# A decode attention layer on one core: the value product as 64 probability columns by 512 V columns in two column groups

## The chip, the cores and the metric

The kernel runs on one core of one Trainium2 chip. The metric is the device time of one execution in microseconds (us); lower is better.

## The reference

One decode step of an adaLN transformer block: 8 batch rows, one token each, model width 512, 32 query heads of width 128 over 8 key/value heads, and a window of W = 2048 cached positions. All data are fp32.

```
mod = (silu(c) @ w_mod) -> sa, ca, ga, sb, cb, gb
h = layernorm(x) * (1 + ca) + sa
q = h @ wq                              # 8 x 32 heads x 128
k, v = last 2048 positions of the caches # 8 x 8 heads x 2048 x 128
p = softmax(q k^T * 128**-0.5)
x = x + ga * ((p v) @ wo)
h = layernorm(x) * (1 + cb) + sb
x = x + gb * (relu(h @ w1 + b1)**2 @ w2 + b2)
```

The caches are large (the windows read are 67 MB of K and 67 MB of V), and each value of them is used for only 4 query heads.

## The kernel before

Everything that comes from DRAM passes through four SBUF slots of 4 MB each. `loads` lists the transfers in order: two pieces of w_mod, two of wq, then for each batch row b the tiles K(b,0), V(b-1,0), K(b,1), V(b-1,1), each 4 key/value heads of one batch row, and at the end wo in two loads, w1 and w2. `pump` issues the next load on SP as soon as a slot is free, and `done` frees a slot: after the scores for a K tile, after the value product for a V tile. The order of work on each engine is the order of the code (a manual schedule), so an instruction that waits holds everything behind it on its engine.

A batch row b goes through these steps, two batch rows overlapping:

- `turn` (line 287, DVE): a K tile is transposed in 32x32 blocks in its slot, in four pieces.
- `scores` (line 297, PE): 16 products for each K tile, stationary 32 columns of the spread queries, moving 512 columns of K, output in column group x of 32 partitions.
- `rows` and `maximum` (lines 309 to 326, DVE): scores to rows, maximum of each head. `exponent` (line 332, ACT): exponentials and their row sums.
- `divisor` (line 344 on PE, line 348 on DVE): the sums of a head over partitions, and their reciprocal rz. `spread` (line 356, ACT): the probabilities times rz, each repeated four times, to prd.
- `turn_p` (line 366 on PE, line 367 on DVE): prd transposed, and masked into pT, where the columns (x, r) of one j hold the 4 query heads r of each of the 4 key/value heads x, and zeros elsewhere.
- `weighted` (line 378 on PE, line 388 on ACT): the value product. A V tile has on each of 128 partitions (x, i) 64 positions j of 128 values. One product takes 32 columns of pT (two positions of 16 columns) as stationary operand and 256 columns of V (the same two positions) as moving operand; the output of 32 x 256 holds the wanted sums where both belong to the same position, and others beside them that are not used. 32 products go in turn to the four column groups of 32 output partitions, eight accumulating in each. ACT copies the result to o_sb.
- `gather` (line 396 on PE, lines 404 and 407 on DVE): products with the selection matrix sel4 add the wanted quarters over partitions and halves u; DVE picks the head's place and adds to oT.

The loop over b calls them as follows (shortened; every `turn` is one of four pieces):

```
turn(b,0,0); divisor(b-1); spread(b-1); gather(b-2); turn(b,0,1)
turn_p(b-1,0..1); turn(b,0,2); turn_p(b-1,2..3); turn(b,0,3)
scores(b,0); weighted(b-1,0)          # for b = 1 in the other order
turn(b,1,0..3); fill(b+1); scores(b,1)
rows(b); maximum(b); exponent(b); weighted(b-1,1)
```

After the last row come the output projection (lines 453 to 472: first half of wo by 512 columns, second half by 128), the second norm (h2T at line 142), the MLP (line 494 with w1, lines 505 to 507, line 516 with w2) and the result (lines 524 to 526). Before the loop stand the modulation (line 221), wq (line 243) and the small constants, sel4 (line 205) among them.

Of the kernel before, what the change touches and what calls it, by code (L numbers as in the profile page):

```python
# [8 lines left out]
F32 = mybir.dt.float32  # L9
# [9 lines left out]
def tile_adaln_cached_attention_mlp(  # L19
# [14 lines left out]
    nc = tc.nc  # L34
    P = 128
# [13 lines left out]
    consts = ctx.enter_context(tc.tile_pool(name="consts", bufs=1))  # L49
    work = ctx.enter_context(tc.tile_pool(name="work", bufs=2))  # L50
    ps_s = ctx.enter_context(tc.tile_pool(name="ps_s", bufs=1, space=bass.MemoryType.PSUM))
    ps_t = ctx.enter_context(tc.tile_pool(name="ps_t", bufs=2, space=bass.MemoryType.PSUM))
    ps_o = ctx.enter_context(tc.tile_pool(name="ps_o", bufs=2, space=bass.MemoryType.PSUM))
# [66 lines left out]
    def done(*keys):  # L120
        for k in keys:
            free.append(held.pop(k))
        pump()
# [4 lines left out]
    one = consts.tile([P, P], F32, name="ident")  # L128
# [4 lines left out]
    sel = consts.tile([P, P], F32, name="sel")  # L133
# [18 lines left out]
    def bank(name="m_ps"):  # L152
        return ps_m.tile([P, 512], F32, name=name, tag="m_ps")
# [47 lines left out]
    nc.vector.tensor_reduce(own, one.rearrange("p (x q r) -> p x r q", x=4, q=4), axis=AX.X, op=ALU.add)  # L201
    same = consts.tile([P, 4, 4, 8], F32, name="same")
    nc.vector.tensor_copy(same, own[:, :, None, :].to_broadcast([P, 4, 4, 8]))
    sel4 = consts.tile([P, 32, 4], F32, name="sel4")
    nc.vector.tensor_copy(sel4, sel[:, :32, None].to_broadcast([P, 32, 4]))
    qb = [consts.tile([P, 32, 4, 8], F32, name=f"qb{i}") for i in range(2)]
    for t in qb:
        nc.gpsimd.memset(t, 0.0)
# [8 lines left out]
    for kc in range(NQ):  # L217
        wm = slot(("mod", kc // 2), 6 * D)[:, kc % 2, :].rearrange("p (m q n) -> p m q n", m=6, q=NQ)
        for i in range(2):
            for q in range(NQ):  # L220
# [4 lines left out]
                    start=(kc == 0),  # L225
                    stop=(kc == NQ - 1),
# [12 lines left out]
    for kc in range(NQ):  # L239
        w = slot(("wq", kc // 2), HQ * DH)[:, kc % 2, :]  # L240
        for t in range(2):
            for x in range(4):
# [4 lines left out]
                    start=(kc == 0),  # L247
                    stop=(kc == NQ - 1),
# [4 lines left out]
    for t in range(2):  # L253
# [3 lines left out]
        for x in range(4):  # L257
# [4 lines left out]
                start=True,  # L262
                stop=True,
# [19 lines left out]
    S_, S2_, NM_, PR_, RZ_, PT_, O_ = ({} for _ in range(7))  # L283
# [88 lines left out]

    def weighted(b, t):
        v = slots[held["V", b, t]]
        o = ps_o.tile([P, 2, P], F32, name="o_ps")
        for m in range(32):
            n, q, u = m // 8, m // 2 % 4, m % 2
            nc.tensor.matmul(  # L378
                o[32 * (m % 4) : 32 * (m % 4) + 32].rearrange("p u d -> p (u d)"),
                PT_[b][:, n, 2 * q + t, 2 * u : 2 * u + 2, :].rearrange("p u r -> p (u r)"),  # L380
                v[:, 256 * m : 256 * m + 256],
                start=(m < 4),
                stop=(m >= 28),
            )
        done(("V", b, t))
        if t == 0:
            O_[b] = work.tile([P, 2, 2, P], F32, name="o_sb")
        nc.scalar.copy(O_[b][:, t], o)  # L388

    def gather(b):  # L390

        o = O_.pop(b)
        pg = bank()
        for t in range(2):
            for u in range(2):
                nc.tensor.matmul(  # L396
                    pg[64 * t : 64 * t + 64, :P],
                    sel4[:, 16 * u : 16 * u + 16, :].rearrange("p n u -> p (n u)"),
                    o[:, t, u, :],
                    start=(u == 0),  # L400
                    stop=(u == 1),
                )
        og = work.tile([P, 4, 32], F32, name="og")
        nc.vector.tensor_mul(  # L404
            og, pg[:, :P].rearrange("p (q i) -> p q i", q=4), m4[:, :, None].to_broadcast([P, 4, 32])
        )
        nc.vector.tensor_reduce(oT[:, :, b], og.rearrange("p q i -> p i q"), axis=AX.X, op=ALU.add)

    for b in range(B + 1):
# [5 lines left out]
        if b > 1:  # L415
            gather(b - 2)
# [12 lines left out]
        if b == 1:  # L429
            weighted(0, 0)  # L430
        if b < B:
            scores(b, 0)
        if b > 1:
            weighted(b - 1, 0)
# [11 lines left out]
        if b > 0:  # L446
            weighted(b - 1, 1)
    gather(B - 1)


    wo_ps = ps_s.tile([P, D], F32, name="s_ps")
    for i in range(16):
# [4 lines left out]
            start=(i < 4),  # L457
            stop=(i >= 12),
# [11 lines left out]
    for i in range(16, 32):  # L470
        for q in range(NQ):
# [4 lines left out]
                start=False,  # L476
                stop=(i == 31),
# [14 lines left out]
    for kc in range(NQ):  # L492
        for g in range(NQ):
# [4 lines left out]
                start=False,  # L498
                stop=(kc == NQ - 1),
            )  # L500
    r = work.tile([P, 32, FC], F32, name="relu", tag="a")
# [12 lines left out]
    for f in range(FC):  # L514
        for q in range(NQ):
# [4 lines left out]
                start=False,  # L520
                stop=(f == FC - 1),
# [41 lines left out]
```

## Time and profile before

| what | value |
|---|---|
| median of 3 runs | 393.99 us (393.91 to 394.86) |
| the profiled execution | 394.03 us, its span in the profile 392.2 us |
| busy: PE, DVE, ACT | 254.6, 213.8, 42.0 us |
| HBM read | 164.77 MB, 420 GB/s over the span |
| value product, line 378 | 1024 instructions, 59.7 us busy |
| scores, line 297 | 512 instructions, 120.9 us busy |
| turning K, line 287 | 64 instructions, 144.0 us busy |

PE is TensorE's matmuls, PEld its weight loads, DVE VectorE, ACT ScalarE, SPq the queue that issues the large loads. A row of the timeline reads: start, duration (both us), engine, line, operation, output<-input, partitions x elements, and in brackets the engine's idle time ahead of it with what ended that. Each fp32 product of the code is two matmul instructions in the profile. A row with x64 merges 64 neighbouring instructions; its duration runs from the first start to the last end. A row that groups a line's instructions (with a bar) has the busy us, the mean ns of one, and the idle time before them. A row with "min/median/max" has one line's durations in ns.

### The profile page before, as it was taken

The numbers are of one execution on the slowest core, as the hardware profiler recorded it, in microseconds if no ns is written. First come the engines' busy times: TensorE is split into PE (matmuls) and PEld (weight loads), VectorE is DVE, ScalarE is ACT, GpSimd is POOL, SyncE is SP. The second block draws the span as 40 slices with busy tenths as digits, with TensorE's granted clock in tenths as the row PEclk, the third lists the DMA queues.
The fourth block names the chain that finished last, engine by engine and source line by source line (L and its number), as shares of the span: only waits on it lengthen the run. The fifth ranks groups of instructions, "written<-read, shape, count | busy, mean of one in ns | idle before, by whom it ended". The sixth has DMA issues, their size and how long they took to land.

```text
span 392.2 us, 4985 instructions
## 1 busy us (share of the span) xinstructions
PE 254.6 (65%) x2224; PEld 112.9 (29%) x2224; DVE 213.8 (55%) x228; ACT 42.0 (11%) x88; POOL 4.7 (1%) x12
## 2 busy tenths in 40 slices
PE   0554808678966693849484939394849384984965
PEld 0211302051231332224332522143224221452423
DVE  2420299399394939283928491939293927230022
ACT  1300100030030002000200120003000300140000
POOL 4000000000000000000000000000000000000000
PEclk9998768969977988789578967797788879997869
DMA  8999999999999999999999999999999999999994
GB/s 333 429 428 426 431 441 438 431 434 438 426 431 426 428 426 428 428 433 434 429 434 433 438 427 428 434 433 428 426 428 434 424 431 426 438 429 412 433 417 170
DMA packets 6997, 165.15 MB, mean 421 GB/s; under 512 B 824, under 2 KB 1088, under 8 KB 1472
## 3 DMA queue, kind: packets, MB, share of 16 engines
q1 hardware_dynamic: 6768, 164.69, 98.1%
q8 instruction: 17, 0.28, 0.3%
q10 hardware_dynamic: 144, 0.13, 0.1%
q14 instruction: 4, 0.03, 0.0%
q0 software_dynamic: 64, 0.01, 0.0%
HBM read 164.77 MB, written 0.07 MB: 420 GB/s over the span
## 4 chain that ended last, share of the span: by engine, by line
DMA 55%; DVE 23%; PE 20%; issue 0%; ACT 0%; DVEq 0%; ACTq 0%
DMA slot<-in_A_k_cache_dram 37%; DVE slot L287 20%; PE s_ps L297 16%; DMA slot<-in_B_w_dram 8%; DMA slot<-in_A_v_cache_dram 6%; DMA xc_in<-in_xc_dram 3%; PE m_ps L221 2%; PE o_ps L378 2%; DVE pT L367 1%; PE t_ps L366 1%; PE t_ps L516 0%; DVE s L309 0%; DVE s L313 0%; DVE mx L318 0%; DVE e_sb L148 0%
## 5 line engine op out<-in xcount | busy, mean ns | idle before, releaser
L287 DVE STREAM_TRANSPOSE slot<-slot 128x2048 f32<-128x2048 f32 x64 | 144.0, 2284 | 43.4 <-DMA slot<-in_A_k_cache_dram 43.3
L297 PE MATMUL s_ps<-slot,qb 128*32 128x512 f32 x512 | 120.9, 1092 | 71.1 <-DVE slot L287 70.5
L297 PEld LDWEIGHTS s_ps<-slot,qb 128*32 128x32 f32 x512 | 24.2, 135 | 147.3 <-issue 79.0
L378 PE MATMUL o_ps<-slot,pT 128*32 128x256 f32 x1024 | 59.7, 381 | 0.8 <-DMA slot<-in_A_v_cache_dram 0.8
L378 PEld LDWEIGHTS o_ps<-slot,pT 128*32 128x32 f32 x1024 | 45.4, 112 | 29.1 <-issue 18.4
L366 PE MATMUL t_ps<-ident,prd 128*128 128x128 f32 x128 | 25.2, 348 | 17.3 <-ACT prd L356 9.5
L309 DVE STREAM_TRANSPOSE s<-s_ps 128x512 f32<-128x512 f32 x8 | 5.7, 717 | 54.1 <-PE s_ps L297 54.1
L366 PEld LDWEIGHTS t_ps<-ident,prd 128*128 128x128 f32 x128 | 18.5, 177 | 23.1 <-ACT prd L356 22.4
L356 ACT ACTIVATE prd<-pr,rz 128x512 f32<-128x512 f32 x32 | 20.5, 710 | 9.4 <-DVE rz L348 9.4
L332 ACT ACTIVATE pr<-s,nm 128x512 f32<-128x512 f32 x8 | 5.8, 722 | 142.7 <-DVE nm L326 142.7
L367 DVE TENSOR_TENSOR pT<-t_ps,m 128x512 f32<-128x512 f32 x32 | 20.2, 670 | 0.7 <-PE t_ps L366 0.6
L388 ACT COPY o_sb<-o_ps 128x256 f32<-128x256 f32 x16 | 5.8, 362 | 121.7 <-PE o_ps L378 121.7
L243 PE MATMUL t_ps<-slot,h1T 128*32 128x512 f32 x64 | 11.6, 889 | 10.2 <-DMA slot<-in_A_wq_dram 10.2
L255 DVE STREAM_TRANSPOSE qT<-t_ps 128x512 f32<-128x512 f32 x2 | 1.4, 717 | 19.0 <-PE t_ps L243 19.0
L274 DVE TENSOR_TENSOR qb<-qrep,block 128x512 f32<-128x512 f32 x8 | 9.0, 1124 | 2.1 <-ACT qrep L266 2.1
L158 PE MATMUL m_ps<-xsum,sel 128*128 128x1 f32 x2 | 0.6, 363 | 13.9 <-DVE xsum L181 13.9
L344 PE MATMUL m_ps<-z,same 128*128 128x1 f32 x16 | 3.3, 273 | 9.1 <-ACT pr L332 9.1
L453 PE MATMUL s_ps<-slot,oT 128*32 128x512 f32 x32 | 5.6, 864 | 5.2 <-DMA slot<-in_A_wo_dram 5.2
L243 PEld LDWEIGHTS t_ps<-slot,h1T 128*32 128x32 f32 x64 | 2.7, 155 | 18.6 <-issue 12.1
L221 PE MATMUL m_ps<-slot,cT 128*32 128x384 f32 x64 | 7.9, 665 | 0.0
L404 DVE TENSOR_TENSOR og<-m_ps,m 128x128 f32<-128x128 f32 x8 | 2.2, 272 | 8.9 <-PE m_ps L396 8.9
L494 PE MATMUL t_ps<-slot,h2T 128*32 128x448 f32 x32 | 5.6, 871 | 2.2 <-DMA slot<-in_B_w_dram 2.2
(93 smaller groups left out, 95.1 us busy)
## 6 DMA issues: line engine op xcount, KB each, us to landing
slot<-in_A_k_cache_dram SPq DMA_DIRECT2D x16, 4096.0 KB, 21.8
slot<-in_A_v_cache_dram SPq DMA_DIRECT2D x16, 4096.0 KB, 25.9
slot<-in_A_wq_dram SPq DMA_DIRECT2D x2, 4096.0 KB, 31.7
slot<-in_w_mod_dram SPq DMA_DIRECT2D x2, 3072.0 KB, 13.9
slot<-in_A_wo_dram SPq DMA_DIRECT2D x1, 4096.0 KB, 22.6
slot<-in_B_w_dram SPq DMA_DIRECT2D x1, 2688.0 KB, 27.8
slot<-in_A_wo_dram SPq DMA_DIRECT2D x1, 2048.0 KB, 25.7
slot<-in_A_wo_dram SPq DMA_DIRECT2D x2, 1024.0 KB, 28.2
```

The lines of the kernel that those rows point to most:

```text
L221: nc.tensor.matmul(pm[i][32 * q : 32 * q + 32, : 3 * P].rearrange("p (m n) -> p m n", m=3), cT[:, kc, :], wm[:, 3 * i : 3 * i + 3, q, :], ...
L243: nc.tensor.matmul(pq[t][32 * x : 32 * x + 32, :], hT[:, kc, :], w[:, 2048 * t + 512 * x : 2048 * t + 512 * x + 512], start=(kc == 0), sto ...
L274: nc.vector.tensor_mul(qb[b % 2][:, :, :, :REP], qrep_b[:, :, None, :, b].to_broadcast([P, 32, 4, REP]), block[:, None, :, None].to_broadc ...
L287: nc.vector.transpose(k, k)
L297: nc.tensor.matmul(S_[b][32 * x : 32 * x + 32, :].rearrange("p (j i) -> p j i", i=8), q[:, n : n + 32], k[:, :, c, :, x], start=(t == 0 an ...
L309: nc.vector.transpose(s1.rearrange("p a j r -> p j a r"), S_.pop(b).rearrange("p (j i) -> p j i", i=32))
L332: nc.scalar.activation(pr.rearrange("p j (a i) -> p j a i", a=4), S2_.pop(b).rearrange("p (a j i) -> p j a i", a=4, i=8), AF.Exp, bias=NM_ ...
L356: nc.scalar.activation(d, pr[:, 4 * n : 4 * n + 4, :, None].to_broadcast([P, 4, 32, 4]), AF.Copy, scale=RZ_[b][0])
L366: nc.tensor.transpose(pp[:, P * i : P * i + P], d[:, i].rearrange("p i u -> p (i u)"), one)
L367: nc.vector.tensor_mul(PT_[b][:, n].rearrange("p q j (x r) -> p q (j x) r", r=REP), pp.rearrange("p (y q r) -> p q y r", y=16, r=REP), m16 ...
L378: nc.tensor.matmul(o[32 * (m % 4) : 32 * (m % 4) + 32].rearrange("p u d -> p (u d)"), PT_[b][:, n, 2 * q + t, 2 * u : 2 * u + 2, :].rearra ...
L388: nc.scalar.copy(O_[b][:, t], o)
```

## The change

A product now takes 64 columns of pT (four positions) and 512 columns of V, and the output goes to one of two column groups of 64 partitions: 16 products for a V tile, eight accumulating in each group. The wanted sums are now a quarter of the output instead of a half. The output and o_sb are twice as wide (o_sb has one buffer for two), and the gather adds four quarters instead of two halves, with a selection matrix sel4 of 64 x 4 columns in place of 32 x 4, made by five DVE instructions instead of one.

```diff
-    sel4 = consts.tile([P, 32, 4], F32, name="sel4")
-    nc.vector.tensor_copy(sel4, sel[:, :32, None].to_broadcast([P, 32, 4]))
+    sel4 = consts.tile([P, 64, 4], F32, name="sel4")
+    nc.vector.tensor_copy(sel4[:, :, 0], one[:, :64])
+    nc.vector.tensor_add(sel4[:, :, 0], sel4[:, :, 0], one[:, 64:])
+    for n in range(1, 4):
+        nc.vector.tensor_copy(sel4[:, :, n], sel4[:, :, 0])
...
-        o = ps_o.tile([P, 2, P], F32, name="o_ps")
-        for m in range(32):
-            n, q, u = m // 8, m // 2 % 4, m % 2
+        o = ps_o.tile([P, 4, P], F32, name="o_ps")
+        for m in range(16):
+            n, q = divmod(m, 4)
             nc.tensor.matmul(
-                o[32 * (m % 4) : 32 * (m % 4) + 32].rearrange("p u d -> p (u d)"),
-                PT_[b][:, n, 2 * q + t, 2 * u : 2 * u + 2, :].rearrange("p u r -> p (u r)"),
-                v[:, 256 * m : 256 * m + 256],
-                start=(m < 4),
-                stop=(m >= 28),
+                o[64 * (m % 2) : 64 * (m % 2) + 64].rearrange("p u d -> p (u d)"),
+                PT_[b][:, n, 2 * q + t].rearrange("p u r -> p (u r)"),
+                v[:, 512 * m : 512 * m + 512],
+                start=(m < 2),
+                stop=(m >= 14),
             )
         done(("V", b, t))
         if t == 0:
-            O_[b] = work.tile([P, 2, 2, P], F32, name="o_sb")
+            O_[b] = work.tile([P, 2, 4, P], F32, name="o_sb", bufs=1)
         nc.scalar.copy(O_[b][:, t], o)
...
-            for u in range(2):
+            for u in range(4):
                 nc.tensor.matmul(
                     pg[64 * t : 64 * t + 64, :P],
                     sel4[:, 16 * u : 16 * u + 16, :].rearrange("p n u -> p (n u)"),
                     o[:, t, u, :],
                     start=(u == 0),
-                    stop=(u == 1),
+                    stop=(u == 3),
                 )
```

No step changes its place. On PE, the steps of one batch row in the loop are these before the change (a name with a number is one buffer; 32x256 is stationary columns x moving columns, and x32 the number of products):

```order
L297 MATMUL s_ps<-slot_84,qb_138 32x512 x16
L378 MATMUL o_ps<-slot_83,pT 32x256 x32
L297 MATMUL s_ps<-slot_81,qb_138 32x512 x16
L378 MATMUL o_ps<-slot_82,pT 32x256 x32
L344 MATMUL m_ps<-z,same 128x1
L396 MATMUL m_ps<-o_sb,sel_136 64x128 x4
L366 MATMUL t_ps<-ident,prd 128x128 x16
```

The first value product stands between the two scores, the second ahead of the divisor, the gather and the transposes. After the change, at the same place:

```order
L301 MATMUL s_ps<-slot_84,qb_142 32x512 x16
L382 MATMUL o_ps<-slot_83,pT 64x512 x16
L301 MATMUL s_ps<-slot_81,qb_142 32x512 x16
L382 MATMUL o_ps<-slot_82,pT 64x512 x16
L348 MATMUL m_ps<-z,same 128x1
L400 MATMUL m_ps<-o_sb,sel_136 64x128 x8
L370 MATMUL t_ps<-ident,prd 128x128 x16
```

The places are the same; the two value products have half as many products of twice the width, and the gather twice as many. Line numbers are four higher from the loop on.

On DVE the stretch behind the maximum is, before the change:

```order
L326 STREAM_TRANSPOSE nm<-mb 128x32
L287 STREAM_TRANSPOSE slot_84<-slot_84 128x2048
L348 RECIPROCAL rz<-m_ps 128x1
L404 TENSOR_TENSOR og<-m_ps,m_127 128x128
L407 TENSOR_REDUCE oT<-og 128x32
L287 STREAM_TRANSPOSE slot_84<-slot_84 128x2048
L367 TENSOR_TENSOR pT<-t_ps,m_130 128x512 x2
```

It is the same after it: the reciprocal waits for the divisor, og for the gather, and the second piece of K is turned behind both.

## The prediction

> **What bounds the kernel now.** First the page: the span, busy time by engine, the slices of DMA.
>
> ```profile
> span 392.2 us, 4985 instructions
> PE 254.6 (65%) x2224; PEld 112.9 (29%) x2224; DVE 213.8 (55%) x228; ACT 42.0 (11%) x88; POOL 4.7 (1%) x12
> DMA  8999999999999999999999999999999999999994
> ```
>
> The DMA slices read 9 from end to end: the 165 MB stream is the bound, and no engine is full. But "full" is an average; the question is how far the compute loop of one batch row is from the stream's period. The chain in order of time, and for its last row the timeline, give that period:
>
> ```profile
> 98.42 7.52 PE s_ps L297 x27
> 126.62 8.90 DVE slot L287 x4
> 283.57 8.90 DVE slot L287 x4
> 292.51 7.62 PE s_ps L297 x22
> 322.44 8.89 DVE L287 STREAM_TRANSPOSE slot<-slot 128x2048 f32<-128x2048 f32 x4 [7.23 <-DMA slot<-in_A_k_cache_dram]
> ```
>
> Line 287 x4 turns the second K tile of a batch row as soon as it lands. From 126.62 to 322.44 are five rows: 39.16 us each, four 4 MB loads of 9.8. Now one loop from the timeline; R is the start of line 309 (scores complete), S that of the next row's first scores:
>
> ```profile
> 260.71 3.81 PE L378 MATMUL o_ps<-slot,pT 128*32 128x256 f32 x64
> 261.12 0.72 DVE L309 STREAM_TRANSPOSE s<-s_ps 128x512 f32<-128x512 f32 x1 [6.78 <-PE s_ps L297]
> 265.08 0.35 ACT L388 COPY o_sb<-o_ps 128x256 f32<-128x256 f32 x1
> 265.23 0.38 PE L344 MATMUL m_ps<-z,same 128*128 128x1 f32 x2 [0.70 <-ACT pr L332]
> 265.54 0.66 PE L396 MATMUL m_ps<-o_sb,sel 128*64 128x128 f32 x8
> 266.50 0.27 DVE L404 TENSOR_TENSOR og<-m_ps,m 128x128 f32<-128x128 f32 x1
> 266.67 2.56 ACT L356 ACTIVATE prd<-pr,rz 128x512 f32<-128x512 f32 x4 [1.24 <-DVE rz L348]
> 266.80 0.38 DVE L407 TENSOR_REDUCE oT<-og 128x32 f32<-128x128 f32 x1
> 267.09 2.30 DVE L287 STREAM_TRANSPOSE slot<-slot 128x2048 f32<-128x2048 f32 x1
> 276.22 7.57 PE L297 MATMUL s_ps<-slot,qb 128*32 128x512 f32 x32 [4.17 <-DVE slot L287]
> 283.47 3.77 PE L378 MATMUL o_ps<-slot,pT 128*32 128x256 f32 x64
> 283.57 8.89 DVE L287 STREAM_TRANSPOSE slot<-slot 128x2048 f32<-128x2048 f32 x4 [7.41 <-DMA slot<-in_A_k_cache_dram]
> 283.84 0.54 SPq L81 DMA_DIRECT2D slot<-in_A_k_cache_dram  x1
> ```
>
> The loop without its wait for DMA: R to S is 276.22 - 261.12 = 15.1; the value product behind the first scores ends at 287.24, S + 11.0, and the second scores can start about there (10.9); they take 7.65. Together 33.65 us, against 39.16: 5.5 us of slack per row, which shows as the 7.41 us that DVE waits for K (part of that wait runs beside PE).
>
> **The change, part by part.** *The value product* (line 378) goes from 32 products of 32 stationary x 256 moving columns, four column groups at a time, to 16 of 64 x 512, two at a time. Each product is two instructions (x64 for 32). The price of a round:
>
> ```profile
> 365.06 0.23 PEld L453 LDWEIGHTS s_ps<-slot,oT 128*32 128x32 f32 x4 [0.63 <-issue]
> 365.81 0.14 PEld L453 LDWEIGHTS s_ps<-slot,oT 128*32 128x32 f32 x4 [0.53 <-issue]
> 366.24 0.13 PEld L453 LDWEIGHTS s_ps<-slot,oT 128*32 128x32 f32 x4 [0.29 <-issue]
> 355.25 0.65 PE L396 MATMUL m_ps<-o_sb,sel 128*64 128x128 f32 x4
> 355.52 0.38 PE L396 MATMUL m_ps<-o_sb,sel 128*64 128x128 f32 x2
> L396 PE MATMUL m_ps<-o_sb,sel x64: 272/273/324, 110.3 to 356.2; 128*64 128x128 f32 x64
> L378 PE MATMUL o_ps<-slot,pT 128*32 128x256 f32 x1024 | 59.7, 381 | 0.8 <-DMA slot<-in_A_v_cache_dram 0.8
> L266 ACT COPY qrep<-m_ps 128x128 f32<-128x128 f32 x8 | 1.5, 280 | 28.5 <-PE m_ps L258 28.3
> L388 ACT COPY o_sb<-o_ps 128x256 f32<-128x256 f32 x16 | 5.8, 362 | 121.7 <-PE o_ps L378 121.7
> ```
>
> Four instructions of 512 columns, one per group, cost 0.43 us at the full granted clock (366.24 - 365.81). In line 378 now four of 256 cost (3.81 - 0.38) / 15 = 0.23, so time goes with moving columns. Does a 64-column group stream as fast, and do two run together? Line 396 is that shape: four instructions of one group alone took 0.65 us (355.25), eight of both groups 0.66 (265.54). So two groups overlap. Two neighbours in one group took 0.38 (355.52) at a median 0.273 each, so they start 0.11 apart: 0.86 ns a column, 0.43 to 0.44 us for 512, as above. A V tile is 32 instructions, 16 rounds of two: 16 x 0.43 + 0.16 = 7.05 us for 3.65, **+3.4 us in each of 16 products**. Half as many products, twice the array time.
>
> *The copy* (line 388) doubles to 512 elements: from 128 to 256 it grew 0.08, so 0.53 for 0.36. *The gather* (line 396) has 8 products: 8 instructions per half instead of 4, +0.44. *sel4* takes five DVE instructions for one, each at most like line 404's 0.27, so 1.1 more in the preamble; there DVE then idles 6.38 us for the modulation product, which hides it (uncovered: +1.1 once).
>
> ```profile
> 23.12 0.56 DVE L231 COPY mod<-m_ps 128x384 f32<-128x384 f32 x1 [6.38 <-PE m_ps L221]
> ```
>
> One buffer for o_sb instead of two costs nothing: the gather that reads it stands on PE ahead of the next product that refills it; without that cover a copy would wait about 0.9 us.
>
> *Where the 3.4 lie.* The second product of a row stands on PE ahead of the divisor and the gather, and DVE holds its next K turn behind both. By the row above: the product ends 264.52 + 3.4 = 267.94; copy to 268.53; rz 268.5, so prd at 268.65 (was 266.67); gather: second half from 268.57 with 8 x 0.109 + 0.2, to 269.65; og and oT to 270.35; the turn that began at 267.09 begins at about 270.3. What follows is DVE work as before, so R to S is 15.1 + 3.2 = 18.3. The first product of a row lies between the two scores: S + 11.0 becomes S + 14.45, and the second scores start at S + 14.3. Loop: 18.3 + 14.3 + 7.65 = 40.25. A switch between 32- and 64-column groups may also expose a pipeline tail: an instruction of line 378 lasts 0.38 where rounds are 0.22 apart, so 0 to 0.19 at each of three switches, 40.8 at most. I take the middle, **40.5 us, over the stream's 39.16**. The compute loop becomes the bound, by 1.3 us a row, after the slack is used up.
>
> The Trainium skill, TensorEngine Tiling (Array Packing), section Key Properties, says that changing the tiling mode drains TensorE; no run here shows a switch between 32 and 64 columns back to back. By that rule the loop is 40.8 and the forecast 1.8 us higher; without it 1.5 lower.
>
> *The sum.* R of row 1 is 105.96 (98.42 + 7.52); there the value product comes ahead of the first scores, and between nothing and all of its 3.4 reaches R, since the second scores wait for DVE too; I take half: 107.65. Six loops of 40.5 bring R of row 7 to 350.65; now it is 322.44 + 8.9 + 7.65 = 339.0. Loads: the slot that the first scores free is refilled from 283.84; the K before it has landed at 283.57 and one V of 9.8 comes between, so the load could come 9.5 later. The lag uses that up at about row 4; from there the stream pauses 1.3 us a row and K still lands about 2 us before DVE wants it. Tail:
>
> ```profile
> 343.76 2.56 ACT L356 ACTIVATE prd<-pr,rz 128x512 f32<-128x512 f32 x4 [0.48 <-DVE rz L348]
> 347.24 3.66 PE L378 MATMUL o_ps<-slot,pT 128*32 128x256 f32 x64
> 356.82 0.37 DVE L407 TENSOR_REDUCE oT<-og 128x32 f32<-128x128 f32 x1
> 361.67 5.61 PE L453 MATMUL s_ps<-slot,oT 128*32 128x512 f32 x32 [5.21 <-DMA slot<-in_A_wo_dram]
> 371.45 1.08 PE L472 MATMUL m_ps<-slot,oT 128*32 128x128 f32 x32 [0.19 <-DMA slot<-in_A_wo_dram]
> 375.80 0.40 DVE L142 STREAM_TRANSPOSE h2T<-h_sb 128x128 f32<-128x128 f32 x1
> 377.95 5.58 PE L494 MATMUL t_ps<-slot,h2T 128*32 128x448 f32 x32 [2.18 <-DMA slot<-in_B_w_dram]
> 385.04 1.95 PE L516 MATMUL t_ps<-slot,rT 128*32 128x128 f32 x64 [1.16 <-DVE rT L507]
> 387.38 1.70 PE L516 MATMUL t_ps<-slot,rT 128*32 128x128 f32 x48 [0.40 <-DMA slot<-in_B_w_dram]
> ```
>
> From R of row 7: prd +7.6 (now 343.76, +4.8), product 3.85 behind it (now 3.48; the longer gather stands ahead of the transposes), two products of 7.0 to +25.4, copy and gather to +27.05, oT +27.8. Now PE has waited for wo, w1 and w2 in turn (5.21, 0.19, 2.18, 0.40); 12 us later all have landed, so the waits go: line 453 in 3.6 (eight rounds of 0.43, its clock no longer cold) +31.4; copies +32.35; lines 467 and 472, 136 x 0.031, +36.5; to h2T 3.65, +40.2; line 494 in 3.2 warm or 5.55 cold, +43.4 to +45.75; relu 1.5; 112 instructions 3.65; last steps 3.1 (392.2 - 389.1): +51.6 to +54.0, middle +52.8. Span 403.4; the profiled run had 394.03 for a span of 392.2, so **405.2 us**, 2.8% slower (the median, 393.99, stands 0.04 from that run).
>
> The Trainium skill, TensorE: Matmul & The Clock Gate, Part 1, says that PE runs at half clock after an idle window of about 3.4 us and at full clock after a busy one; line 453's rounds agree (0.75 from 365.06 to 365.81, 0.43 after it). By that rule line 494 comes after about 3.7 us of little PE work and may go either way.
>
> **Rivals.** (1) *The slots' lead holds; no change* (393.5 to 395.2). For: DMA reads 9 throughout and the loop has 5.5 us of slack. For R of row 7 to be within 1.6 of now the loop must be at most (340.6 - 107.65) / 6 = 38.8 us; it grows by two products, so each may grow 2.7, not 3.4: rounds of 0.385 us. Neither row of that shape (0.43, 0.44) allows it, but a wait that I put on the chain wrongly, 1.5 us a row, would. The tail alone, with no lag, ends at 339 + 52.8 = 391.8, hidden. (2) *The loop ends near the stream*, 39.2 to 40: the first rows' lag stays or grows slowly, R of row 7 at 343 to 347.5, time 397 to 402. Speaks for it: the divisor and gather may finish sooner than I stack them. (3) *Faster*: the stream gains from fewer PE reads of weights. It must run over 0.3% faster while the lag is absorbed; the DMA slices show 9 beside busy and idle PE alike. About 391.5. (4) *Worse*: the drained switches and late loads bind together, K landing after S, each us of landing delay counting a row: above 408.5.
>
> **How the numbers follow.** Loop as worked out (402 to 408.5) 0.66; rival 2 0.16; rival 1 0.10; rival 4 0.05; faster 0.03. The range takes rival 2's upper part and the bounds of the switches and the clock: 398 to 408.5. A difference under 0.3% (1.2 us) can hardly be told from none; slower 0.87, same 0.10, faster 0.03.
>
> **What would show it.** Line 382 at some 7.0 us per V tile in 32 x 2 x 8 = 512 instructions; starts of line 313 (now 309) about 40.5 apart; the second K turn no longer waiting for DMA from row 3 on; DMA slices below 9 in the second half; no DMA wait before the last weights. Wrong if a 64-column round is not 0.43, if the turn behind the gather slips by less than 2.5 us, or if K lands late.

## The result and the profile after

The changed kernel takes 406.59 us (median of 4 runs, 405.88 to 407.02), the kernel before 393.95: ratio 1.0314, 95% interval 1.0291 to 1.0337. The prediction was 405.2 (398.0 to 408.5). The profiled execution took 405.88 for a span of 404.0.

The page of the changed kernel, the lines that answer to those of before with the chain's shares, and its groups for turning K, the value product and the gather (busy us and mean ns behind the bar):

```profile
span 404.0 us, 4100 instructions
PE 306.4 (76%) x1776; PEld 106.4 (26%) x1776; DVE 215.6 (53%) x232; ACT 46.1 (11%) x88; POOL 4.7 (1%) x12
DMA  8999999999999899999998999899989998999993
PE 66%; DVE 19%; DMA 11%; ACT 1%; issue 1%; DVEq 0%; ACTq 0%
...
L291 DVE STREAM_TRANSPOSE slot<-slot 128x2048 f32<-128x2048 f32 x64 | 143.9, 2284 | 5.5 <-DMA slot<-in_A_k_cache_dram 5.5
L382 PE MATMUL o_ps<-slot,pT 128*64 128x512 f32 x512 | 114.0, 598 | 0.0
L400 PE MATMUL m_ps<-o_sb,sel 128*64 128x128 f32 x128 | 13.0, 278 | 0.0
```

In the kernel before, the chain's shares and the group of line 287 were:

```profile
DMA 55%; DVE 23%; PE 20%; issue 0%; ACT 0%; DVEq 0%; ACTq 0%
L287 DVE STREAM_TRANSPOSE slot<-slot 128x2048 f32<-128x2048 f32 x64 | 144.0, 2284 | 43.4 <-DMA slot<-in_A_k_cache_dram 43.3
```

PE is still only 76% busy, yet the chain that ended last is now 66% PE and 11% DMA (before: 55% DMA), and the DMA slices show 8s, the first from 131 to 141 us, the others in the second half: the stream pauses. DVE's wait for K ahead of its turns fell from 43.3 to 5.5 us. The value product went from 59.7 to 114.0 us busy with half the instructions.

One loop of the chain in order of time (start, us, what; row 2 to row 3), then from the timeline the score transposes of rows 2, 3 and 7 and the copy of a product:

```profile
149.00 7.03 PE o_ps L382 x32
156.04 0.31 PE m_ps L348 x2
156.35 1.52 PE m_ps L400 x16
157.90 0.30 DVE og L408
158.22 0.38 DVE oT L411
158.60 2.22 DVE slot L291
...
165.38 2.23 DVE slot L291
167.65 7.51 PE s_ps L301 x29
175.16 7.02 PE o_ps L382 x32
182.18 7.47 PE s_ps L301 x26
```

```profile
149.08 0.72 DVE L313 STREAM_TRANSPOSE s<-s_ps 128x512 f32<-128x512 f32 x1 [11.25 <-PE s_ps L301]
156.08 0.59 ACT L392 COPY o_sb<-o_ps 128x512 f32<-128x512 f32 x1 [2.96 <-PE o_ps L382]
189.72 0.72 DVE L313 STREAM_TRANSPOSE s<-s_ps 128x512 f32<-128x512 f32 x1 [10.45 <-PE s_ps L301]
352.67 0.72 DVE L313 STREAM_TRANSPOSE s<-s_ps 128x512 f32<-128x512 f32 x1 [13.58 <-PE s_ps L301]
```

No piece of this loop in the chain is DMA. Both value products stand in it, each 7.0 us: one ahead of the divisor and the gather for which DVE waits, one between the scores. From 149.08 to 352.67 are five loops of 40.72 us; the stream's own period is 39.16.

### The profile page after: what moved, and what is told of

Its sections match the earlier page's. It is cut to its first block, busy times and chain, and to the rows that moved or that the text cites. A ratio compares the mean times of both kernels' runs of the same rounds, so it can differ in the third digit from the quotient of the medians.

```text
span 404.0 us, 4100 instructions
## 1 busy us (share of the span) xinstructions
PE 306.4 (76%) x1776; PEld 106.4 (26%) x1776; DVE 215.6 (53%) x232; ACT 46.1 (11%) x88; POOL 4.7 (1%) x12
## 4 chain that ended last, share of the span: by engine, by line
PE 66%; DVE 19%; DMA 11%; ACT 1%; issue 1%; DVEq 0%; ACTq 0%
PE o_ps L382 28%; PE s_ps L301 28%; DVE slot L291 13%; DMA slot<-in_A_k_cache_dram 9%; DVE pT L371 3%; PE m_ps L400 3%; DMA xc_in<-in_xc_dram 3%; PE m_ps L225 2%; PE t_ps L370 1%; PE s_ps L457 1%; PE m_ps L476 1%; PE t_ps L520 1%; ACT prd L360 1%; PE t_ps L498 1%; DVE oT L411 1%
## 5 line engine op out<-in xcount | busy, mean ns | idle before, releaser
L382 PE MATMUL o_ps<-slot,pT 128*64 128x512 f32 x512 | 114.0, 598 | 0.0
L382 PEld LDWEIGHTS o_ps<-slot,pT 128*64 128x64 f32 x512 | 35.5, 138 | 89.1 <-issue 89.1
L370 PE MATMUL t_ps<-ident,prd 128*128 128x128 f32 x128 | 21.2, 308 | 18.4 <-DVE pT L371 16.0
L392 ACT COPY o_sb<-o_ps 128x512 f32<-128x512 f32 x16 | 9.4, 588 | 183.1 <-PE o_ps L382 183.1
L370 PEld LDWEIGHTS t_ps<-ident,prd 128*128 128x128 f32 x128 | 15.5, 155 | 22.8 <-issue 19.7
L400 PE MATMUL m_ps<-o_sb,sel 128*64 128x128 f32 x128 | 13.0, 278 | 0.0
L400 PEld LDWEIGHTS m_ps<-o_sb,sel 128*64 128x64 f32 x128 | 11.1, 136 | 0.7 <-issue 0.6
L352 DVE RECIPROCAL rz<-m_ps 128x1 f32<-128x1 f32 x8 | 1.3, 163 | 15.7 <-PE m_ps L348 15.7
L225 PE MATMUL m_ps<-slot,cT 128*32 128x384 f32 x64 | 6.9, 595 | 0.0
```

Source lines behind the costliest of these rows:

```text
L225: nc.tensor.matmul(pm[i][32 * q : 32 * q + 32, : 3 * P].rearrange("p (m n) -> p m n", m=3), cT[:, kc, :], wm[:, 3 * i : 3 * i + 3, q, :], ...
L370: nc.tensor.transpose(pp[:, P * i : P * i + P], d[:, i].rearrange("p i u -> p (i u)"), one)
L382: nc.tensor.matmul(o[64 * (m % 2) : 64 * (m % 2) + 64].rearrange("p u d -> p (u d)"), PT_[b][:, n, 2 * q + t].rearrange("p u r -> p (u r)" ...
L400: nc.tensor.matmul(pg[64 * t : 64 * t + 64, :P], sel4[:, 16 * u : 16 * u + 16, :].rearrange("p n u -> p (n u)"), o[:, t, u, :], start=(u = ...
```

## Experiments

The theory (1): array time, 3.4 us in each of two products of a loop with 5.5 us of slack, so that together they make the loop longer than the stream's period. Loops below are distances between starts of the score transposes.

**Twice the array time in the old form.** Every value product of the kernel before is issued twice:

```diff
-        for m in range(32):
+        for m in list(range(32)) * 2:
```

> The kernel before with each value product issued twice over (the second pass starts the sums anew): 64 products of 32 x 256 per V tile, so the array time of the change without its wider copy, longer gather or switches between 32- and 64-column groups. Theory 1 (array time of both products on a loop that has 5.5 us of slack): 7.1 us a tile, loop 39.8 to 40.0 us, time 399 (398 to 401). Rival 2 (copy, gather and group switches are what costs): loop stays 39.2, time 394 to 395.5.

Measured: 400.72 us, ratio 1.0167 (1.0147 to 1.0187). From its timeline:

```profile
146.68 7.17 PE L378 MATMUL o_ps<-slot,pT 128*32 128x256 f32 x128
147.02 0.72 DVE L309 STREAM_TRANSPOSE s<-s_ps 128x512 f32<-128x512 f32 x1 [10.11 <-PE s_ps L297]
164.80 7.57 PE L297 MATMUL s_ps<-slot,qb 128*32 128x512 f32 x32 [4.88 <-DVE slot L287]
186.68 0.72 DVE L309 STREAM_TRANSPOSE s<-s_ps 128x512 f32<-128x512 f32 x1 [9.88 <-PE s_ps L297]
```

A tile takes 7.17 us and the loop 39.66, just under the 39.8 to 40.0 expected; the time lies within the expected 398 to 401. By the medians the array time alone gives about half of the loss (6.8 of 12.6 us); rival 2, that copy, gather and switches do it alone, falls. But this loop is only 0.5 us over the stream's period, and that of the changed kernel is 1.06 us longer still, so the array time is not the whole of it: once it has used up the slack, copy, gather and switches count in full. No run takes these three apart. By the rows of one loop, 0.79 lies on the way from R to S (17.78 here, 18.57 in the changed kernel, where the copy and the longer gather lie) and 0.19 from S to the next R (21.88 here, 189.72 - 167.65 = 22.07 there, with two switches of group width).

**One wide product a row.** The first tile only, or the second only, in the new form; the other, and its part of the gather, as before:

```diff
     def weighted(b, t):
+        if t != WIDE:        # WIDE = 0 or 1
+            narrow(b, t)     # 32 products of 32 x 256, as before
+            return
```

> 64 x 512 products for the first V tile of a row only (the one between the two scores), 32 x 256 for the second. Theory 1: the loop grows to 37.3 us, still under the stream's 39.2, so nothing is seen: 394 to 395.5. Rival 3 (each wide product costs its share of the 12.6 us, whatever the loop's slack): 400.

> 64 x 512 products for the second V tile of a row only (the one ahead of the divisor and the gather). Theory 1: loop 37.1 us, under 39.2, 394 to 395.5. Rival 3: 400. Rival 4 (only the product ahead of the divisor matters): 402 to 406 here and 394 with the first alone.

Measured: 394.42 (ratio 1.0013, 1.0002 to 1.0023) and 394.37 (1.0012, 1.0002 to 1.0021). Either half of the change costs a tenth of a per cent, the whole of it 3.1%. The costs don't add, so rivals 3 and 4 fall. The run with the first tile wide shows why, in the score transposes of rows 1 and 2 and in the turns of rows 2 to 5:

```profile
108.81 0.72 DVE L313 STREAM_TRANSPOSE s<-s_ps 128x512 f32<-128x512 f32 x1 [8.95 <-PE s_ps L301]
146.19 0.72 DVE L313 STREAM_TRANSPOSE s<-s_ps 128x512 f32<-128x512 f32 x1 [9.29 <-PE s_ps L301]
```

```profile
127.01 8.89 DVE L291 STREAM_TRANSPOSE slot<-slot 128x2048 f32<-128x2048 f32 x4 [2.98 <-DMA slot<-in_A_k_cache_dram]
166.25 8.89 DVE L291 STREAM_TRANSPOSE slot<-slot 128x2048 f32<-128x2048 f32 x4 [4.77 <-DMA slot<-in_A_k_cache_dram]
205.10 8.89 DVE L291 STREAM_TRANSPOSE slot<-slot 128x2048 f32<-128x2048 f32 x4 [6.23 <-DMA slot<-in_A_k_cache_dram]
243.95 8.89 DVE L291 STREAM_TRANSPOSE slot<-slot 128x2048 f32<-128x2048 f32 x4 [7.03 <-DMA slot<-in_A_k_cache_dram]
```

While it is late the loop runs at 37.38 us (37.3 expected); it catches up with the stream, and then DVE waits for K again, longer each row.

**All of the work, off the chain.** The changed kernel with its second product in two parts, the second part where PE idles behind the transposes, and the gather behind the first scores:

```diff
             turn_p(b - 1, 3)
+        if b > 1:
+            weighted(b - 2, 1, 8, 16)
...
             scores(b, 0)
         if b > 1:
+            gather(b - 2)
             weighted(b - 1, 0)
...
-            weighted(b - 1, 1)
+            weighted(b - 1, 1, 0, 8 if b < B else 16)
```

> The changed kernel's products, but the second product of a row cut in two: eight products where they were, eight behind the transposes of the next probabilities, where PE idles; the gather goes behind the next first scores, its DVE part behind the turns. All of the work is done. Theory 1: the way from R to S returns to about 15, loop 37.9, so the stream bounds again: 394 to 396. Rival 5 (the PE time itself or the later release of V slots costs, wherever it stands): 403 to 407.

Measured: 396.46 (395.26 to 397.42), ratio 1.0073 (1.0053 to 1.0094); 10 of the 12.6 us are back with the same products. Its score transposes of rows 2 and 3, and a turn of row 5:

```profile
145.95 0.72 DVE L313 STREAM_TRANSPOSE s<-s_ps 128x512 f32<-128x512 f32 x1 [8.70 <-PE s_ps L301]
184.33 0.72 DVE L313 STREAM_TRANSPOSE s<-s_ps 128x512 f32<-128x512 f32 x1 [7.48 <-PE s_ps L301]
```

```profile
244.06 8.89 DVE L291 STREAM_TRANSPOSE slot<-slot 128x2048 f32<-128x2048 f32 x4 [7.26 <-DMA slot<-in_A_k_cache_dram]
```

Its first scores of the next row start at 161.00, so R to S is 15.0 (about 15 expected); the loop is 38.4 us (expected 37.9), under the stream's, and DVE waits for K again. Rival 5, PE time or the later release of V slots wherever it stands, falls: here the second V slot is released later still. But 396.46, the median of runs from 395.26 to 397.42, lies just above the 394 to 396 expected.

**The rest of it.** The same with the last batch row in the old form:

```diff
     def weighted(b, t, lo=0, hi=16):
+        if b == B - 1:
+            narrow(b, t)
+            return
```

> The run with the second product cut in two, its last batch row done by products of 32 x 256 as in the kernel before (the other seven rows stay 64 x 512). If what was left there over the kernel before (396.5 against 393.9) is the two long products behind the last row: 393.7 to 394.4. If it is the loop: 396 to 397.

Measured: 395.39 (394.99 to 395.71), ratio 1.0036 (1.0021 to 1.005), between the two times expected. The ends of the two in the chain, the split run first, then this one:

```profile
380.86 4.72 PE t_ps L513 x32
387.06 3.31 PE t_ps L535 x112
```

```profile
358.75 29.57 DMA slot<-in_B_w_dram
388.37 1.74 PE t_ps L558 x48
```

With the long products at the end PE finishes last; without them it waits again for w2. So the two long products at the end gave 1.1 of the 2.5 us by the medians; the remaining 1.5 was expected at 0.5 at most. In the profiled executions 1.0 of it stands in the last landing of w2 (the product behind it starts at 388.37, in the kernel before at 387.38). Why the stream ends 1 us later there stays open.

**Less DMA.** Both kernels loading half of each V tile (the other half of the slot keeps old data):

```diff
-            nc.sync.dma_start(t, v)
+            if kind == "V":
+                nc.sync.dma_start(t[:, : NJ * DH // 2], v[:, :, : NJ * DH // 2])
+            else:
+                nc.sync.dma_start(t, v)
```

> The kernel before, loading only half of each V tile (the other half of the slot holds old data), which takes a quarter off the loop's DMA (29.4 us a row). Theory 1: the compute loop shows itself at 33.7 us a row, time 352 to 356. If the loop has no such length of its own (DMA bound throughout): 29.4 us a row, about 320.

> The changed kernel, loading only half of each V tile. Theory 1: loop still 40.7 us, time 402 to 406. Rival 6 (late slots starve the stream and the stream sets the time): well below, 330 to 395.

Measured, one run each: 355.08, within the 352 to 356 expected, and 407.18, over the 402 to 406. Score transposes of rows 1 and 2 of the first and of rows 3 and 4 of the second, from the timelines; behind each the DMA slices of its page:

```profile
106.21 0.72 DVE L312 STREAM_TRANSPOSE s<-s_ps 128x512 f32<-128x512 f32 x1 [6.60 <-PE s_ps L300]
139.66 0.72 DVE L312 STREAM_TRANSPOSE s<-s_ps 128x512 f32<-128x512 f32 x1 [8.69 <-PE s_ps L300]
```

```profile
DMA  8999999996798839995998599789959995999994
```

```profile
189.27 0.72 DVE L316 STREAM_TRANSPOSE s<-s_ps 128x512 f32<-128x512 f32 x1 [12.59 <-PE s_ps L304]
229.96 0.72 DVE L316 STREAM_TRANSPOSE s<-s_ps 128x512 f32<-128x512 f32 x1 [12.40 <-PE s_ps L304]
```

```profile
DMA  8999999947994699369936993699369945699950
```

The changed kernel's loop is 40.69 with a quarter of its stream gone and DMA idling: it isn't the stream that sets it, nor late slots (rival 6). Its time is over the expected because its end is longer, not its loop: the product with w1 took 4.95 us there, in the changed kernel's profiled execution 3.26. The kernel before drops to 33.45 in this loop: that is the hidden compute loop, forecast at 33.65. (From row 3 on DVE waits for K again, 2.1 to 2.5 us a row, and the later loops are 33.6 to 34.1, so the loop before these waits is the one to read.)

**Order of the column groups.** The first eight products of a tile in one group, the last eight in the other:

```diff
-                o[64 * (m % 2) : 64 * (m % 2) + 64]
+                o[64 * (m // 8) : 64 * (m // 8) + 64]
```

> The changed kernel, with the first eight products of a tile all in one column group and the last eight in the other, instead of in turn. If PE starts instructions of different groups out of order without limit: 406. If it looks ahead only a little, the groups run one after the other: up to 14 us a tile, loop up to 54.7 us, time up to 505.

Measured: 487.97 (one run). A tile in its timeline:

```profile
245.94 12.29 PE L382 MATMUL o_ps<-slot,pT 128*64 128x512 f32 x32
```

12.29 us is 28 rounds of 0.43 and a tail of 0.25, where 16 rounds would be full overlap and 32 none. The starts in the trace show which four rounds are shared: instructions of the first group start at 251.14, 251.57, 252.00 and 252.43, the first four of the second at 251.15, 251.63, 252.06 and 252.49; all the others start alone, 0.43 apart. Two rows of the weight loads show the change from pairs to single ones:

```profile
252.00 0.20 PEld L382 LDWEIGHTS o_ps<-slot,pT 128*64 128x64 f32 x2 [0.23 <-issue]
252.49 0.14 PEld L382 LDWEIGHTS o_ps<-slot,pT 128*64 128x64 f32 x1 [0.29 <-issue]
```

So in this run products of two groups ran together only where they stood close in the order. (The expectation of the next run speaks of three instructions; it is four.)

**The gather's order.** The changed kernel with the gather's products in turn over the groups:

```diff
-        for t in range(2):
-            for u in range(4):
+        for u in range(4):
+            for t in range(2):
```

> The changed kernel, its gather's products in turn over the two column groups (t inside u) instead of all of one half first. In the run with the groups in blocks only the last three instructions of a group overlapped the next group's, and the changed kernel's gather takes 1.52 us. If the groups then overlap throughout: gather 1.1 to 1.2 us, loop 40.3 to 40.5, time 403.5 to 405.5. If the wait for the copy sets it: 406.6 as before.

Measured: 406.56 (ratio 1.0319, 1.0304 to 1.0334), no change; its gather still takes 1.53:

```profile
196.05 1.53 PE L400 MATMUL m_ps<-o_sb,sel 128*64 128x128 f32 x16
196.49 0.85 PEld L400 LDWEIGHTS m_ps<-o_sb,sel 128*64 128x64 f32 x14 [0.25 <-ACT o_sb L392]
```

That is what was expected if the wait for the copy sets its end, and the second row shows that wait: two weight loads go ahead, and the other 14 start only once the copy to o_sb is done (begun at 195.85, 0.58 long). From there the two groups do run side by side, their instructions 0.01 us apart in pairs, but the eight of the second half still follow each other 0.1 us apart, so nothing is gained.

## Why the prediction was right, point by point

- **The bound and the slack.** Right. The compute loop under the stream was put at 33.65 us by adding rows along the chain; with less DMA it showed at 33.45.
- **The price of a product.** Right: 7.03 for 7.05, from a round of 0.43 and the doubling by two groups for four.
- **Copy and gather.** The copy took 0.59 (forecast 0.53); the gather ends 1.2 behind the copy (156.35 + 1.52 against 156.06 + 0.59), where 1.1 was forecast. R to S is 18.57 for 18.3.
- **Switches of group width.** Taken as 0 to 0.19 each. Two of them lie between S and the next R, which is 0.19 longer than in the doubled run; that run has about the same array time and no switch there, so 0.19 is an estimate of what the two cost together. The traces show the wait: behind the scores the first wide product starts 0.01 to 0.07 us before the last score instruction ends, in the doubled run 0.18 to 0.41 before. The Trainium skill, TensorEngine Tiling (Array Packing), section Key Properties, has TensorE drained at such a switch. These starts agree with it, but the cost is about half of the full tail by which the prediction priced the rule.
- **The loop and the lag.** 40.72 for 40.5; R of row 7 at 352.67 for 350.65. In row 1, scores end at 108.14 for 107.65: of the 3.4 us, 2.2 reached them, where the prediction took half without working it out.
- **The tail.** 404.0 - 352.67 = 51.3, just below the 51.6 to 54.0. The end of the chain of the changed kernel, behind the scores of row 1:

```profile
93.30 14.84 PE s_ps L301 x57
...
364.16 13.88 PE o_ps L382 x64
380.66 3.67 PE s_ps L457 x32
392.85 3.26 PE t_ps L498 x32
397.58 3.31 PE t_ps L520 x112
```

  The product with w1 took 3.26 us for 5.58 before: the lower of the two bounds (3.2 and 5.55) between which the prediction took the middle. With the last products, 3.31 for 3.65, it gave back 1.5 of the 2.0 us by which row 7 was later than forecast. So the total is nearer than its terms, and in part by luck. The w1 product ran at a granted TensorE clock of 1.00 in this execution; in the doubled run, the changed kernel with half of V, and the two runs on the order of products it took 4.95 us at 0.65 to 0.66. In the run with the gather's order changed:

```profile
391.66 4.95 PE t_ps L498 x32
```

- **What was not right.** K was to land 2 us before DVE wants it, and its second turn was to stop waiting from row 3 on. DVE's turns still waited 5.5 us for it in all (the group of line 291), 4.3 of them in rows 2, 3 and 6. The stream was to pause only from about row 4; the first 8 of the DMA slices stands at 131 to 141 us, ahead of R of row 2. The late K cost nothing, because PE holds the second scores until S + 14.5 while turning takes 8.9. That the tail alone, without lag, would hide (391.8) was not tested: the split run has no lag, but half a product and the gather of row 6 stand in its tail.

## What to carry to other kernels

A kernel whose DMA slices are full from end to end still has a compute loop with a length of its own: add it up along the chain, without its waits for DMA, and a change costs next to nothing up to the difference (0.1% here) and counts in full, every loop, beyond it. Two edits that are each nearly free can together cost 3%, so test them together. Before widening an fp32 product to more stationary columns, count the moving columns times the groups that no longer run beside each other; where the longer work must stay, look for the engine's idle stretch first, as the split run did.

## What the runs showed of the hardware

Column groups overlapped only within a short distance in the order of the products: with 16 instructions of one group ahead of 16 of the other (one run), four overlapped and a tile took 12.29 us instead of 7.03. The first of the second group started at 251.15 and so ahead of the last three of the first, which stand before it in the order. In the kernel before, a gather half of four instructions hid wholly beside the other half (0.66 us for eight), which had not shown that there is such a limit.
